# K^T V in column halves, states in quarters of the array, and weight rows loaded to match

## The chip, the cores and the metric

One core of one Trainium2 chip. The metric is the device time of one execution in microseconds (us), as the median of several runs.

## The reference

Eight batches of eight heads, 576 positions, head size 64: causal attention without softmax and with a decay per head, whose output, laid out as 4608 tokens of 512, goes through three up-projections with an elementwise maximum and one down-projection.

```python
scores = q @ k.T / sqrt(64)
ret = scores * where(i >= j, gamma[h] ** (i - j), 0)      # i, j positions
x = (ret @ v)                                            # heads side by side: 4608 x 512
h = maximum(maximum(x @ w1, x @ w2), x @ w3)             # 4608 x 768
out = h @ w_out                                          # 4608 x 512
```

The four weight matrices come as 64-bit floats; the kernel turns them into 32-bit ones itself.

## The kernel before

Tokens are cut into 36 chunks of 128 (`g`). For each chunk the kernel makes scores, multiplies them by the mask, multiplies with the decayed values `vd`, and adds the state of the earlier chunks times the queries. The state is a running sum of K^T V. Four chunks are a tile of 512 tokens for the projections (`up`, `downs`, in Strassen's form of seven products instead of eight). The attention of tile t+1 is spread over the projections of tile t.

```python
def state(g):                     # K^T V of a pair of heads as one 128x128 product
    ...
    kv = ps_r.tile([P, NP, P], FP32, tag="r", name="kv")
    for p in range(NP):           # NP = 4 pairs of heads
        nc.tensor.matmul(kv[:, p, :], lhsT=pair(kr, p)[r:], rhs=pair(vds[g], p)[r:], ...)     # L205
    ...                           # VectorE: + old state; GpSimd: * gs (which zeroes the off-diagonal blocks)

def values(*chunks):
    ...
    for p in range(NP):           # two heads beside each other in column halves
        for j in range(2):
            nc.tensor.matmul(o[g][D * j:D * (j + 1), p, :], lhsT=vr[:, 2 * p + j, :], rhs=st[:, j, p, :], ...)  # L226
    ...
            for p in range(NP):   # block-diagonal state of a pair, whole array
                nc.tensor.matmul(o[g][:, p, :old], lhsT=sd[:, p, :], rhs=qT[:, p, :old], ...)  # L234
    ...
def load_weights(n):
    ...
    nc.sync.dma_start(t[:].rearrange("p (dc f) -> p dc f", f=P),                               # one transfer a piece
                      WS[i][:, fb * P:(fb + 1) * P].rearrange("(dc p) f -> p dc f", p=P))
    ...
# in the steps of a tile, for each two chunks a, b:
at(m + 3, (state, a))
at(m + 4, (state, b))
at(m + 5, (values, a, b))
```

## Time and profile before

| | before |
|---|---|
| time | 820.41 us, median of 3 (819.88 to 820.86) |
| span in the profile | 818.6 us |
| stage 1, until the last weight is converted | 0 to 108.6 us |
| stage 2, to the end | 710.0 us |
| VectorE busy in 20.6 to 108.6 us | 86.7 of 88.0 us |
| granted clock | 1.00 throughout |

Two kinds of time are used. "Busy" is the time from an instruction's start to its end; for matmuls it contains latency and adds up to more than passes. "Start to start" is the time from a group's first start to the next group's first start; it is what the group costs in a full queue. A "record" is one matmul as the trace shows it; each product of 32-bit floats leaves two. The "mode" of the array is how it is divided: whole (128*128 in the lines), in column halves (128*64), row halves (64*128) or quarters (64*64). An "evacuation" is the operation that takes a result out of the bank of PSUM, the memory that matmuls write to, and so frees it. The prediction shows the lines of the profile on which both rest.

### The profile page before, as it was taken

How to read it: one execution, taken by the hardware profiler on the slowest of the kernel's cores; microseconds unless marked ns; L12 is line 12 of the kernel's file. 1: busy time of each engine (PE TensorE's matmuls, PEld its weight loads, DVE VectorE, ACT ScalarE, POOL GpSimd, SP SyncE). 2: the span in 40 equal slices, each digit the busy share in tenths (PEclk: the TensorE clock that was granted, in tenths of full speed). 3: DMA queues.
4: the chain of work that ended last, by engine and by line, in shares of the span. 5: the costliest groups of instructions: out<-in, count | busy, mean ns of one | idle time of the engine just before them, and what ended most of it. 6: DMA issues, size and time to landing. Idle time of an engine off the chain costs nothing.

```text
span 818.6 us, 12678 instructions
## 1 busy us (share of the span) xinstructions
PE 811.4 (99%) x4616; PEld 670.1 (82%) x4616; DVE 432.6 (53%) x805; ACT 173.7 (21%) x401; POOL 190.9 (23%) x182
## 2 busy tenths in 40 slices
PE   8999999999999999999999999999999999999998
PEld 7555457888888888888888888888888888888887
DVE  3999997454454535354445345553545344533341
ACT  2766521111111111110111111111111021111211
POOL 3645486112211130113021122102111302111000
PEclk9999999999999999999999999999999999999999
DMA  9966522333232323332224313333333232001001
GB/s 233 284 199 173 131 58 63 56 60 72 66 57 53 58 72 66 57 57 56 60 54 79 64 52 57 55 57 87 56 54 56 66 73 52 1 14 39 1 1 51
DMA packets 236094, 59.33 MB, mean 72 GB/s; under 512 B 217088, under 2 KB 234496, under 8 KB 236032
## 3 DMA queue, kind: packets, MB, share of 16 engines
q1 hardware_dynamic: 235888, 58.53, 32.0%
q8 instruction: 36, 0.59, 0.3%
q14 instruction: 26, 0.21, 0.1%
q10 hardware_dynamic: 144, 0.00, 0.0%
HBM read 49.03 MB, written 9.44 MB: 71 GB/s over the span
## 4 chain that ended last, share of the span: by engine, by line
PE 86%; DVE 6%; issue 2%; SPq 2%; DMA 2%; ACT 1%; POOL 0%; DVEq 0%; ACTq 0%
PE x L461 31%; PE z L461 15%; PE dx L334 10%; PE y L461 8%; PE dz L334 5%; PE o L226 3%; PE s L191 3%; PE o L234 3%; PE kv L205 3%; PE dy L334 3%; PE down L510 2%; DVE expo L413 2%; DVE frac L402 1%; SPq L160 1%; DVE mant L408 1%
## 5 line engine op out<-in xcount | busy, mean ns | idle before, releaser
L461 PE MATMUL x<-S,T 128*128 128x256 f32 x576 | 147.9, 379 | 0.0
L461 PEld LDWEIGHTS x<-S,T 128*128 128x128 f32 x576 | 109.1, 190 | 15.4 <-ACT u L466 0.3
L211 POOL TENSOR_TENSOR state<-state,gs 128x512 f32<-128x512 f32 x24 | 32.2, 1341 | 241.2 <-DVE state L210 237.3
L461 PE MATMUL x<-xT,w 128*128 128x256 f32 x288 | 75.6, 385 | 0.0
L491 DVE TENSOR_TENSOR tmp<-x,p 128x256 f32<-128x256 f32 x48 | 20.4, 424 | 102.8 <-PE x L461 102.8
L461 PE MATMUL x<-S,w 128*128 128x256 f32 x288 | 74.3, 380 | 0.0
L461 PE MATMUL y<-xT,w 128*128 128x256 f32 x288 | 73.9, 379 | 0.0
L461 PE MATMUL z<-S,w 128*128 128x256 f32 x288 | 73.9, 379 | 0.0
L461 PE MATMUL z<-xT,T 128*128 128x256 f32 x288 | 73.9, 379 | 0.0
L312 POOL TENSOR_TENSOR H<-h 128x256 f32<-128x256 f32 x24 | 20.5, 856 | 226.9 <-DVE h L504 226.9
L466 ACT COPY p<-x 128x256 f32<-128x256 f32 x72 | 26.8, 372 | 202.3 <-PE x L461 202.3
L519 PE MATMUL up<-xT,w 128*128 128x512 f32 x144 | 63.5, 595 | 0.2 <-POOL w L419 0.2
L238 DVE TENSOR_TENSOR xT<-o,gq 128x512 f32<-128x512 f32 x36 | 24.5, 689 | 69.9 <-PE o L234 63.9
L461 PEld LDWEIGHTS y<-xT,w 128*128 128x128 f32 x288 | 54.7, 190 | 7.4
L461 PEld LDWEIGHTS z<-S,w 128*128 128x128 f32 x288 | 54.7, 190 | 7.4
L461 PEld LDWEIGHTS z<-xT,T 128*128 128x128 f32 x288 | 54.5, 189 | 7.7
L461 PEld LDWEIGHTS x<-S,w 128*128 128x128 f32 x288 | 49.4, 189 | 13.2 <-issue 1.5
L461 PEld LDWEIGHTS x<-xT,w 128*128 128x128 f32 x288 | 52.1, 190 | 8.0 <-issue 0.5
L519 PEld LDWEIGHTS up<-xT,w 128*128 128x128 f32 x144 | 26.7, 190 | 31.4 <-issue 30.6
L194 DVE TENSOR_TENSOR st<-s,causal 128x512 f32<-128x512 f32 x72 | 44.9, 682 | 8.2 <-PE s L191 7.3
L466 ACT COPY u<-x 128x256 f32<-128x256 f32 x72 | 26.8, 372 | 100.2 <-PE x L461 95.7
L480 DVE TENSOR_TENSOR tmp<-y,p 128x256 f32<-128x256 f32 x48 | 20.4, 424 | 45.3 <-PE y L461 39.3
(92 smaller groups left out, 1218.9 us busy)
## 6 DMA issues: line engine op xcount, KB each, us to landing
bits<-in_moe_w_dram SPq DMA_DIRECT2D x18, 512.0 KB, 5.1
out_dram<-osb SPq DMA_DIRECT2D x35, 256.0 KB, 2.1
kraw<-in_k_dram SPq DMA_DIRECT2D x32, 256.0 KB, 3.0
vraw<-in_v_dram SPq DMA_DIRECT2D x32, 256.0 KB, 3.5
qraw<-in_q_dram SPq DMA_DIRECT2D x464, 16.0 KB, 1.8
kxraw<-in_k_dram SPq DMA_DIRECT2D x464, 16.0 KB, 1.8
bits<-in_moe_w_out_dram SPq DMA_DIRECT2D x6, 512.0 KB, 4.8
qraw<-in_q_dram SPq DMA_DIRECT2D x6, 256.0 KB, 5.6
```

Of the source, the lines that this page charges most:

```text
L191: nc.tensor.matmul(s[j][:, p, :], lhsT=kT[r, p, :], rhs=qT[r, p, :], start=True, stop=True)
L194: nc.vector.tensor_tensor(st[:, j], s[j][:], masks[start_of(g)][:].unsqueeze(1).to_broadcast([C, NP, C]), op=ALU.mult)
L205: nc.tensor.matmul(kv[:, p, :], lhsT=pair(kr, p)[r:], rhs=pair(vds[g], p)[r:], start=True, stop=True)
L211: nc.gpsimd.tensor_tensor(t[:], t[:], gs[:], op=ALU.mult)
L226: nc.tensor.matmul(o[g][D * j:D * (j + 1), p, :], lhsT=vr[:, 2 * p + j, :], rhs=st[:, j, p, :], start=(p == 0), stop=(before(g) == 0 and p ...
L234: nc.tensor.matmul(o[g][:, p, :old], lhsT=sd[:, p, :], rhs=qT[:, p, :old], start=False, stop=(p == NP - 1), skip_group_check=True)
L238: nc.vector.tensor_tensor(xT[t][:, :, i * C:(i + 1) * C], o[g][:], gq[:], op=ALU.mult)
L312: chores.append(lambda: (pool(s3, a11, a21, op=ALU.subtract), pool(s4, a12, s2, op=ALU.subtract)))
L334: nc.tensor.matmul(out[m], lhsT=hS[n](fp)[:, m * P:(m + 1) * P], rhs=late["T"][n][:, fp, :], start=first and fp == 0 and (m == 0 or last a ...
L461: nc.tensor.matmul(out[:], lhsT=w[:, d * P:(d + 1) * P], rhs=xS[t][n][:, d, :], start=first and d == 0, stop=d == 1, skip_group_check=True)
L466: nc.scalar.copy(c[:], src[:])
L519: nc.tensor.matmul(ps[:], lhsT=w_sb[i, fb][:, dc * P:(dc + 1) * P], rhs=xT[t][:, dc, :], start=(dc == 0), stop=(dc == NDC - 1))
```

## The change

Its intent: only the diagonal blocks of K^T V are wanted, and of the block-diagonal state half is zeros, so TensorE does twice the work needed. Per head, K^T V fits half of the array's columns, so two heads run side by side, and it is put directly behind the values, which use the same halves. The state times the queries is 64 by 64 per head, a quarter of the array, so four heads could run at once. For that, heads of both row halves must come to lie in each column half; the order of rows of x changes, and with it the rows of the three up weights and of the decay tables.

```diff
+    def state(g):
+            for h in range(H):
+                nc.tensor.matmul(kvs[g][half(h % 2), h // 2, :], lhsT=kr[r:, h, :], rhs=vds[g][r:, h, :], ...)
...
+    def head(c, n):
+        return NP * c + (n ^ c)
...
+        o = [pool.tile([P, len(chunks), NP // 2, C], FP32, tag=tag, name="o") for _ in range(2)]
+        (values: o[n % 2][half(c), m, n // 2, :] with h = head(c, n))
+        for g in new_states:
+            state(g)
-                    nc.tensor.matmul(o[g][:, p, :old], lhsT=sd[:, p, :], rhs=qT[:, p, :old], ...)
+                for n in range(NP):
+                    for c in range(2):
+                        h = head(c, n)
+                        r = half(h % 2)
+                        nc.tensor.matmul(o[n % 2][half(c), m, n // 2, :old], lhsT=states[g][r, h // 2, :],
+                                         rhs=qks[g]["q"][r, h // 2, :old], ...)
...
-                nc.sync.dma_start(t[:].rearrange("p (dc f) -> p dc f", f=P), ...)
+                for c, n in ((0, slice(0, NP)), (1, slice(0, NP, 2)), (1, slice(1, NP, 2))):
+                    h = slice(0, NP) if c == 0 else slice(head(c, n.start), H, 2)
+                    nc.sync.dma_start(blocks[half(c), n], heads[:, h])
...
+    def tables():                 # were two transfers, are six
+        for j in range(2):
+            yield gs[half(j)], state_decay[half(j), :, half(j)]
+        for c in range(2):
+            for b in range(2):
+                yield gq[half(c), b::2, :], out_decay[half(b ^ c), NP // 2 * c:NP // 2 * (c + 1), :]
...
-    state(0)                      # and so for chunks 1 to 3
-    values(0)
+    values([0], [0])
...
-            at(m + 3, (state, a))
-            at(m + 4, (state, b))
-            at(m + 5, (values, a, b))
+            at(m + 4, (decay_values, a + 2))
+            at(m + 5, (values, [a, b], [b, a + 2]))
```

(Cut: the smaller state and its evacuation `keep`, pool sizes, the passing of arguments.)

More of the change, by code (lines that the diff above doesn't have):

```diff
@@ L82 @@
     att = ctx.enter_context(tc.tile_pool(name="att", bufs=2))
-    stp = ctx.enter_context(tc.tile_pool(name="stp", bufs=3))
+    stp = ctx.enter_context(tc.tile_pool(name="stp", bufs=4))
     xpool = ctx.enter_context(tc.tile_pool(name="xpool", bufs=2))
@@ L98 @@
     gq = const.tile([P, NP, C], FP32, name="gq")
-    gs = const.tile([P, NP, P], FP32, name="gs")
+    gs = const.tile([P, NP, D], FP32, name="gs")
     nc.scalar.dma_start(gk[:], key_decay)
@@ L124 @@
         nc.gpsimd.memset(m[0:r, r:C], 0.0)
-    raws, vds, qks, sts, states = {}, {}, {}, {}, {}
+    raws, vds, qks, sts, states, kvs = {}, {}, {}, {}, {}, {}
     def spans(g):
@@ L156, in load @@
                 for t, what in between:
-                    nc.sync.dma_start(t[:], what)
+                    nc.sync.dma_start(t, what)
             t = raws[n, g] = raw.tile([C, H, D], FP32, tag=n, name=n + "raw", bufs=4 if n == "k" else 3)
@@ L195, in scores, with begins, half @@
                                     op=ALU.mult)
+    def begins(g):
+        return g + 1 < NG and start_of(g + 1) != 0
+    def half(j):
+        return slice(D * j, D * (j + 1))
     def state(g):
-        kr = raws.pop(("k", g))
-        if g + 1 == NG or start_of(g + 1) == 0:
-            return
-        r = start_of(g) or 0
-        kv = ps_r.tile([P, NP, P], FP32, tag="r", name="kv")
-        for p in range(NP):
-            nc.tensor.matmul(kv[:, p, :], lhsT=pair(kr, p)[r:], rhs=pair(vds[g], p)[r:], start=True, stop=True)
@@ L206, in state @@
-        t = states[g + 1] = stp.tile([P, NP, P], FP32, tag="state", name="state")
-        if start_of(g) is not None:
-            nc.vector.tensor_tensor(t[:], kv[:], gs[:], op=ALU.mult)
-        else:
-            nc.vector.tensor_tensor(t[:], kv[:], states[g][:], op=ALU.add)
-            nc.gpsimd.tensor_tensor(t[:], t[:], gs[:], op=ALU.mult)
+        kr = raws["k", g]
+        if begins(g):
+            r = start_of(g) or 0
+            pool, tag = (ps_r, "r") if g >= CPT else (ps_x, "x")
+            kvs[g] = pool.tile([P, NP, D], FP32, tag=tag, name="kv")
+            for h in range(H):
+                nc.tensor.matmul(kvs[g][half(h % 2), h // 2, :], lhsT=kr[r:, h, :], rhs=vds[g][r:, h, :],
+                                 start=True, stop=True)
@@ L213, with keep @@
+    def keep(g):
+        if begins(g):
+            kv = kvs.pop(g)
+            t = states[g + 1] = stp.tile([P, NP, D], FP32, tag="state", name="state")
+            if start_of(g) is not None:
+                nc.vector.tensor_tensor(t[:], kv[:], gs[:], op=ALU.mult)
+            else:
+                nc.vector.tensor_tensor(t[:], kv[:], states[g][:], op=ALU.add)
+                nc.gpsimd.tensor_tensor(t[:], t[:], gs[:], op=ALU.mult)
     xT, xS = {}, {}
-    def values(*chunks):
+    def head(c, n):
+        return NP * c + (n ^ c)
@@ L218, in before, with values @@
+    def values(chunks, new_states=()):
         def before(g):
             return C if start_of(g) is None else start_of(g)
-        o = {g: ps_r.tile([P, NP, C], FP32, tag="r", name="o") for g in chunks}
-        for g in chunks:
-            st, vr = sts.pop(g), vds.pop(g)
-            for p in range(NP):
-                for j in range(2):
-                    nc.tensor.matmul(o[g][D * j:D * (j + 1), p, :], lhsT=vr[:, 2 * p + j, :], rhs=st[:, j, p, :],
-                                     start=(p == 0), stop=(before(g) == 0 and p == NP - 1), skip_group_check=True)
@@ L228, in values @@
-        for g in chunks:
-            t, i = divmod(g, CPT)
-            qT, old = qks.pop(g)["q"], before(g)
-            if old > 0:
-                sd = states.pop(g)
-                for p in range(NP):
-                    nc.tensor.matmul(o[g][:, p, :old], lhsT=sd[:, p, :], rhs=qT[:, p, :old],
-                                     start=False, stop=(p == NP - 1), skip_group_check=True)
-            if i == 0:
-                xT[t] = xpool.tile([P, NDC, NT], FP32, tag="xT", name="xT")
-            nc.vector.tensor_tensor(xT[t][:, :, i * C:(i + 1) * C], o[g][:], gq[:], op=ALU.mult)
+        t, i = divmod(chunks[0], CPT)
@@ new lines, in values @@
+        pool, tag = (ps_r, "r") if t > 0 else (ps_y, "y")
+        o = [pool.tile([P, len(chunks), NP // 2, C], FP32, tag=tag, name="o") for _ in range(2)]
+        for m, g in enumerate(chunks):
+            for n in range(NP):
+                for c in range(2):
+                    h = head(c, n)
+                    nc.tensor.matmul(o[n % 2][half(c), m, n // 2, :], lhsT=vds[g][:, h, :],
+                                     rhs=sts[g][:, h % 2, h // 2, :], start=m == 0 and n < 2,
+                                     stop=before(g) == 0, skip_group_check=True)
@@ new lines, in values @@
+        for g in new_states:
+            state(g)
+        for m, g in enumerate(chunks):
+            old = before(g)
+            if old > 0:
+                for n in range(NP):
+                    for c in range(2):
+                        h = head(c, n)
+                        r = half(h % 2)
+                        nc.tensor.matmul(o[n % 2][half(c), m, n // 2, :old], lhsT=states[g][r, h // 2, :],
+                                         rhs=qks[g]["q"][r, h // 2, :old], start=False, stop=True,
+                                         skip_group_check=True)
@@ new lines, in values @@
+        if i == 0:
+            xT[t] = xpool.tile([P, NDC, NT], FP32, tag="xT", name="xT")
+        for b in range(2):
+            shape = [P, NP // 2, len(chunks), C]
+            nc.vector.tensor_tensor(
+                xT[t][:, b::2, i * C:(i + len(chunks)) * C].rearrange("p u (m c) -> p u m c", c=C),
+                o[b][:].rearrange("p m u c -> p u m c"), gq[:, b::2, :].unsqueeze(2).to_broadcast(shape), op=ALU.mult)
+        for g in new_states[:1]:
+            keep(g)
+        i += len(chunks) - 1
@@ L276, in load_weights @@
             else:
-                nc.sync.dma_start(t[:].rearrange("p (dc f) -> p dc f", f=P),
-                                  WS[i][:, fb * P:(fb + 1) * P].rearrange("(dc p) f -> p dc f", p=P))
+                heads = WS[i][:, fb * P:(fb + 1) * P].rearrange("(h p) f -> p h f", p=D)
+                blocks = t[:].rearrange("p (n f) -> p n f", f=P)
+                for c, n in ((0, slice(0, NP)), (1, slice(0, NP, 2)), (1, slice(1, NP, 2))):
+                    h = slice(0, NP) if c == 0 else slice(head(c, n.start), H, 2)
+                    nc.sync.dma_start(blocks[half(c), n], heads[:, h])
     late, chores = {}, deque()
@@ L557, in ffn @@
         yield
+    def tables():
+        for j in range(2):
+            yield gs[half(j)], state_decay[half(j), :, half(j)]
+        for c in range(2):
+            for b in range(2):
+                yield gq[half(c), b::2, :], out_decay[half(b ^ c), NP // 2 * c:NP // 2 * (c + 1), :]
     warm(6)
     load(0)
-    load(1, (gs, state_decay), (gq, out_decay))
+    load(1, *tables())
     load(2)
@@ L572 @@
     scores(0)
-    state(0)
     transposes(1)
-    values(0)
+    values([0], [0])
     decay_values(2)
     scores(1)
-    state(1)
     transposes(2)
-    values(1)
+    values([1], [1])
     decay_values(3)
     scores(2)
-    state(2)
     transposes(3)
     convert(2)
-    values(2)
+    values([2], [2])
     convert(2)
     scores(3)
-    state(3)
     decay_values(4)
     convert(2)
-    values(3)
+    values([3], [3])
     transposes(4)
@@ L601, in at @@
         def at(n, *what):
-            todo[n].extend(partial(step, *args) for step, *args in what if args[0] < NG)
+            for step, *args in what:
+                if step is values:
+                    if args[0][0] < NG:
+                        todo[n].append(partial(values, args[0], [g for g in args[1] if g < NG]))
+                elif args[0] < NG:
+                    todo[n].append(partial(step, *args))
         if t == 1:
@@ L606, in steps @@
             at(0, (load, b))
-            at(1, (scores, a), (state, a))
+            at(1, (scores, a), (state, a), (keep, a))
             at(2, (transposes, b), (decay_values, b), (load, c))
             at(3, (scores, b), (load_blocks, d, 0))
-            at(4, (state, b), (load_blocks, d, 1, 2))
-            at(5, (values, a, b), (load_blocks, d, 3), (load, d))
-            at(6, (transposes, c), (decay_values, c), (load_blocks, d + 1, 0))
+            at(4, (decay_values, c), (load_blocks, d, 1, 2))
+            at(5, (values, [a, b], [b, c]), (load_blocks, d, 3), (load, d))
+            at(6, (keep, c), (transposes, c), (load_blocks, d + 1, 0))
             at(7, (transposes, d), (decay_values, d), (load_blocks, d + 1, 1, 2))
             at(8, (scores, c), (scores, d), (load_blocks, d + 1, 3), (load, d + 1))
-            at(9, (state, c), (load_blocks, d + 2, 0, 1))
-            at(10, (state, d), (load_blocks, d + 2, 2))
-            at(11, (values, c, d), (load_blocks, d + 2, 3), (load, d + 2))
+            at(9, (load_blocks, d + 2, 0, 1))
+            at(10, (decay_values, d + 1), (load_blocks, d + 2, 2))
+            at(11, (values, [c, d], [d, d + 1]), (load_blocks, d + 2, 3), (load, d + 2))
             return todo
@@ L620, in steps @@
             a, b, m = CPT * t + n, CPT * t + n + 1, 6 * (n // 2)
-            at(m, (transposes, a), (decay_values, a), (load, a + 2))
+            at(m, (keep, a), (transposes, a), (load, a + 2))
             at(m + 1, (transposes, b), (decay_values, b))
             at(m + 2, (scores, a), (scores, b), (load, b + 2))
-            at(m + 3, (state, a))
-            at(m + 4, (state, b))
-            at(m + 5, (values, a, b))
+            at(m + 4, (decay_values, a + 2))
+            at(m + 5, (values, [a, b], [b, a + 2]))
         return todo
```

## The prediction

> **What bounds the kernel now.** I read the page first (busy shares, the 40 slices), then busy time by stage, the waits of TensorE, and last the matmul timeline at the places that the diff touches.
>
> ```profile
> PE 811.4 (99%) x4616; PEld 670.1 (82%) x4616; DVE 432.6 (53%) x805; ACT 173.7 (21%) x401; POOL 190.9 (23%) x182
> ...
> DVE  3999997454454535354445345553545344533341
> ```
>
> TensorE is busy for the whole span, but VectorE is full in the slices of roughly 20 to 130 us. The table by stage (stretch, its length, busy time of PE, PEld, DVE, ACT, POOL) makes it sharper:
>
> ```profile
> 20.00:108.00 88.00, 86.92 (x378) 46.34 (x374) 86.21 (x128) 55.72 (x85) 46.79 (x31) 1.00 0.69 187
> 108.00:130.00 22.00, 21.33 (x95) 11.79 (x96) 21.44 (x26) 1.76 (x3) 21.01 (x23) 1.00 0.29 74
> 130.00:818.60 688.60, 685.64 (x3977) 596.13 (x3975) 317.65 (x639) 110.76 (x305) 115.77 (x115) 1.00 0.26 53
> ```
>
> So there are two stages. Up to about 108 us, VectorE converts the 64-bit weights (86.2 of 88.0 us) and TensorE has to wait for what it makes; a faster TensorE gains nothing there. From 108 us on nothing holds TensorE back. The waits of the matmul row from 108 us to the end are one line:
>
> ```profile
> PE down L510 <- POOL w_out L419: 0.8, 1, 0.8
> ```
>
> The end is therefore set by how many array slots the second stage fills, about 706 us from 108.6 us on when I add up start-to-start times. I price everything by start-to-start, since a busy figure of a pipelined matmul (379 ns for one that starts every 216) is latency. In the timeline the next group's start closes a group; a matmul on 32-bit floats is two records, each with its own weight load:
>
> ```profile
> 156.27 1.05 PE L205 MATMUL kv<-vd,kraw 128*128 128x128 f32 x8
> 157.16 1.03 PE L461 MATMUL x<-xT,w 128*128 128x256 f32 x4
> ...
> 162.99 0.38 PE L461 MATMUL x<-S,w 128*128 128x256 f32 x1
> 163.30 1.97 PE L226 MATMUL o<-st,vd 128*64 128x128 f32 x32
> 165.20 1.16 PE L234 MATMUL o<-qT,state 128*128 128x128 f32 x8
> 166.19 0.38 PE L461 MATMUL x<-xT,w 128*128 128x256 f32 x1
> ```
>
> The reader is to see three prices. K^T V (L205): 8 records in 0.89 us, 111 ns each. Values in column halves (L226): 32 records in 1.90 us, 59 ns each; the single records show pairs 6 to 7 ns apart, one pair every 109 ns, so two halves really run at once. States with queries (L234) on the whole array: 8 in 0.99 us, and 16 in 1.89 us for two chunks. And a price for changing the array's shape: the full matmul before L226 takes 310 ns to the next start in place of 216 (+94), the first pair of L226 lasts 160 ns in place of 109 (+51), and L226 to L234 costs +93 and then +101.
>
> **What the Trainium skill says.** (1) "TensorEngine Tiling (Array Packing)", Tiling Modes, Key Properties: a change of tiling mode drains TensorE, while tiles of one mode load and multiply independently. The trace agrees: the 94 to 200 ns just named for a change, and pairs 7 ns apart within a mode. (2) "TensorE: Matmul & The Clock Gate", LDWEIGHTS: the load takes columns / 1.2 ns and does not depend on rows. In the load rows
>
> ```profile
> L226 PEld LDWEIGHTS o<-st,vd 128*64 128x64 f32 x576 | 31.2, 137 | 7.8 <-issue 6.5 <-DVE st L194 1.1 <-DVE state L210 0.2
> L234 PEld LDWEIGHTS o<-qT,state 128*128 128x128 f32 x256 | 30.0, 191 | 3.3 <-issue 3.3
> ```
>
> 128 columns cost 54 ns more than 64, as the page gives, and loads of 128 columns start every 111 to 112 ns. So L205 and L234 are paced by loads as much as by matmuls. (3) The same page, Back-to-back issue gap: columns / 2.4 + 2.5 ns, and a floor of about 25 ns per matmul. For these two-pass floats the trace has 216 ns at 256 columns and 109 at 128, which is the formula with two cycles a column; for 64 I take 56 to 57 ns. The floor has no witness in this trace: nothing here runs faster than 55 ns per record. (4) "TensorEngine Tiling", Gotcha 1: row tiles must not be in one PSUM bank at once. The diff obeys it: head(c, n) sends the two row halves that meet in one column half to two different banks.
>
> **The change part by part, in the second stage.**
>
> K^T V. Removed: 25 groups of 8 in the second stage (22.85 us by start-to-start: 22 at 0.891 and 3 half-chunk ones at 1.085). Of the full product only the two diagonal head blocks were ever used. Added: 16 records per chunk of 64 columns in and 64 out, two column halves side by side. A pair costs 57 ns by either load or matmul; 8 pairs are 0.456 us, and 25 chunks 11.4 us. They stand behind L226, in the same mode, so they add no change of shape. Gain **11.4 us**.
>
> States with queries. Removed: 15 groups in the second stage, 25.5 us (9 of 1.89, 3 of 1.835, 3 of 0.995). Added: twice the records, each in a quarter of the array. Four successive heads take four different quarters, so four records should share a 109 ns slot: 16 records a chunk are 4 slots, 0.437 us. 27 chunks give 11.8 us, less 3 x 0.21 for the chunks of which only 64 queries need a state, plus about 0.1 us at each of 15 entries: 12.7 us. Gain **12.8 us**.
>
> The price of quarters: the way out. L234 used to be in the same mode as the matmuls behind it; now there is one more change in each of 15 calls. Scores (L191), which also leave a tiled mode for the full array, show it:
>
> ```profile
> 142.09 2.06 PE L191 MATMUL s<-qT,kT 64*128 64x128 f32 x32
> 144.08 1.13 PE L461 MATMUL x<-xT,w 128*128 128x256 f32 x4
> ```
>
> The four L461 behind them take 0.967 us to the next start in place of 0.863, and the last score pair some 0.1 more: 0.2 us x 15 = **3.0 us lost**.
>
> Sum: 11.4 + 12.8 - 3.0 = 21.2 us.
>
> Other engines. The state's addition and scaling shrink from 512 to 256 columns (VectorE 687 ns towards the 424 that its 256-column additions take; GpSimd 1341 towards half). Neither is on the path after 108 us. Evacuations are again two of 512 columns per two chunks, but both now wait for the last of both chunks; that delays the sums for the next tile by 0.7 us or so. Those are wanted about 8 us later, so this is free. K^T V is taken a step earlier or later, with a whole up-projection unit (6 us) for its 1.07 us of decayed values.
>
> First stage. VectorE loses 0.26 us for each of some 7 states and pays 0.16 more for each of the first 4 evacuations (two of 256 columns for one of 512): about 1 us won, where it is full. Against it stands the transfer queue: 6 table transfers in place of 2, 3 for each of 18 weight pieces in place of 1, and an issue takes at least 0.43 us:
>
> ```profile
> 4.90 0.85 SPq L157 DMA_DIRECT2D gs<-in_state_decay_dram  x1
> 5.79 0.43 SPq L157 DMA_DIRECT2D gq<-in_out_decay_dram  x1
> ...
> 14.13 2.74 SPq L277 DMA_DIRECT2D bits<-in_moe_w_dram  x2
> ...
> 23.11 6.46 SPq L277 DMA_DIRECT2D bits<-in_moe_w_dram  x6
> ```
>
> Four more tables are +1.5 us of issue, but the queue stalls for 2.75 us right after them, with the transfer engines full, so most is absorbed, and 128 KB less is moved. A weight piece now costs 3 x 0.47 = 1.4 us to issue against the 1.1 to 1.4 us seen, so the first pieces come at most a microsecond later. Net of the stage: 0, give or take 1.5 us. 820.4 - 21.2 is 799.2; I state **800**, rounding towards a few unpriced fill slots.
>
> **The rivals.** (a) Quarters do not overlap fourfold. If loads or issue let only two records share a slot, L234 costs 8 slots a chunk, as before, and the extra change of mode makes that part a loss of 3 us: 820.4 - 11.4 + 3 = 812. For it: no four-way overlap and nothing under 55 ns per record is in this trace; a call now puts 96 matmuls and 96 loads in a row, where L226 had 32 and 32, so records may be issued too slowly (four loads and four matmuls per 109 ns are 14 ns each, where L226 needed 27). Against it: halves overlap perfectly by columns (L226) and by rows (L191), and starts 6 to 7 ns apart leave room for eight records in 109. (b) Only K^T V disappoints, since its matmuls are half as long: if a pair stays at 109 ns, its gain is 0 and the time 811. Against it: the second pair of loads of L226 starts 55 ns after the first. (c) The first stage grows: later weights delay VectorE, which is the bound there, and every lost microsecond stays. If all the added issue before the first weights were exposed, +2 to +4 us: 802 to 804. The 2.75 us stall speaks against it. (d) A new wait at the values call (K^T V before decayed values, or PSUM's four shared banks now holding two outputs and two states): 0.5 us in each of 15 calls would be +7, so 807. All their producers have most of a unit's 6 us, so I hold it unlikely.
>
> **Range and chances.** Faster by over 2% needs less than 804.0. The main path (both overlaps work) has 0.65 to 0.7 and ends at 797 to 803; (a) or (b) has about 0.2 and ends at 808 to 812; (c) and (d) push a little more over 804. Slower than 836 would need a failure of a kind I see no sign of. Range 796 to 811; faster 0.66, same 0.31, slower 0.03.
>
> **What would show it.** K^T V at about 28 ns per record start-to-start, 0.46 us per chunk; L234's successor at about 27 ns per record, 1.0 us per two chunks; each call still followed by a slow first full matmul (0.1 us more); TensorE's waits after 108 us still near 0; the first `down` still at about 103 us and the rest of the program 21 us shorter. Wrong if the records of quarters sit at 55 ns, if K^T V pairs stay near 109, if waits for a state, for decayed values or for a PSUM buffer appear on TensorE, or if the conversion of weights ends later than before.

## The result, and the profile after

The changed kernel takes 806.97 us (median of 4, 804.83 to 808.08) against 820.23 us (median of 4, 819.88 to 820.86). The ratio is 0.9834, 95% interval 0.9811 to 0.9858: better by 1.7%, short of 2%. Ratios here are the mean time of one kernel's runs over the mean of the other's of the same rounds, so they are not quite the ratio of the quoted medians.

The array did what was hoped. One values call for two chunks, in the matmul timeline of the kernel before (columns: start, duration to the last end, engine, line, operation, tile, count):

```profile
204.79 1.97 PE L226 MATMUL o<-st,vd 128*64 128x128 f32 x32
206.69 2.05 PE L234 MATMUL o<-qT,state 128*128 128x128 f32 x16
208.58 0.38 PE L334 MATMUL dx<-To,H 128*128 128x256 f32 x1
```

and the same call after:

```profile
207.48 1.97 PE L244 MATMUL o<-st,vd 128*64 128x128 f32 x32
209.28 1.10 PE L211 MATMUL kv<-vd,kraw 128*64 128x64 f32 x32
210.31 1.10 PE L256 MATMUL o<-qT,state 64*64 64x128 f32 x32
211.35 0.48 PE L367 MATMUL dx<-To,H 128*128 128x256 f32 x1
```

Read starts against starts. K^T V of two chunks takes 1.03 us (209.28 to 210.31), where it took 2 x 0.89. States take 1.04 us (210.31 to 211.35) against 1.89. In the single records, K^T V goes in pairs 6 to 7 ns apart every 58 ns, and the states go four at a time, 6 to 7 ns apart, every 109 ns.

The stages of the kernel after (stretch, length, busy time of PE, PEld, DVE, ACT, POOL with counts, granted clock, DMA share, GB/s) show where the rest went:

```profile
23.00:113.00 90.00, 84.04 (x430) 43.41 (x422) 85.26 (x132) 55.41 (x84) 48.48 (x32) 0.98 0.74 182
113.00:134.60 21.60, 21.58 (x118) 11.03 (x119) 19.82 (x25) 1.76 (x3) 19.92 (x22) 0.93 0.34 82
134.60:803.10 668.50, 665.40 (x4369) 575.57 (x4367) 305.96 (x639) 110.76 (x305) 105.00 (x114) 1.00 0.27 55
```

| us, profiled runs | before | after | difference |
|---|---|---|---|
| VectorE starts converting weights | 20.63 | 22.91 | +2.3 |
| last weight converted (end of stage 1) | 108.62 | 112.96 | +4.3 |
| first matmul of the Strassen products | 129.86 | 134.60 | +4.7 |
| from the first Strassen product to the end | 688.7 | 668.5 | -20.2 |
| span | 818.6 | 803.1 | -15.5 |

So the array gained 20.2 us from the first Strassen product on, and the start gave 4.7 back. Three things are new in the start. The first is the transfer queue, in the timeline of its issues:

```profile
5.28 1.52 SPq L157 DMA_DIRECT2D gs<-in_state_decay_dram  x2
6.84 2.56 SPq L157 DMA_DIRECT2D gq<-in_out_decay_dram  x4
...
17.26 4.12 SPq L311 DMA_DIRECT2D bits<-in_moe_w_dram  x6
...
26.88 11.83 SPq L311 DMA_DIRECT2D bits<-in_moe_w_dram  x18
```

The two tables took 1.33 us to issue and now take 4.1; the first weights are issued at 17.26 us, not 14.13; the next six pieces take 11.8 us, not 6.5. The second is a wait of VectorE inside the conversion, in its timeline (in brackets the idle time before it and its cause):

```profile
31.33 0.76 DVE L263 TENSOR_TENSOR xT<-o,gq 128x256 f32<-128x256 f32 x2 [2.96 <-PE o L256]
```

The third is the clock. The kernel before was granted 1.00 all along. This one has two stretches of 3.4 us at half of it, called slow stretches below:

```profile
27.50:30.90 3.40, 3.30 (x41) 3.13 (x44) 0.87 (x3) 1.44 (x2) 1.03 (x2) 0.50 0.80 202
112.80:116.20 3.40, 3.18 (x4) 1.50 (x5) 3.13 (x5) 0.58 (x1) 2.86 (x5) 0.50 0.21 32
```

The second of these lies in stage 2, where TensorE sets the end: 3.4 us at half speed costs an estimated 1.7. The experiments bear this out: from the conversion's end to the first Strassen product, the profiled runs without a slow stretch there (e1, e6, e8, e12) take 20.06 to 20.12 us, those with one (the change, e2, e3, e5) 21.44 to 21.76. The first lies on the work that VectorE waits for at 28 to 31 us. The Trainium skill ("TensorE: Matmul & The Clock Gate", Part 1: The HAM clock gate) says that the clock halves after an idle window of about 3.4 us and that windows run freely; the length of 3.4 us and the share of 0.50 agree. I had read it and saw no reason to use it, since nothing in the trace before was throttled.

### The profile page after: what moved, and what is told of

Same layout as the page of the kernel before. It is cut to its first block, busy times and chain, and to the rows that moved or that the text cites. A ratio compares the mean times of both kernels' runs of the same rounds, so it can differ in the third digit from the quotient of the medians.

```text
span 803.1 us, 13762 instructions
## 1 busy us (share of the span) xinstructions
PE 789.4 (98%) x5128; PEld 646.0 (80%) x5128; DVE 417.4 (52%) x809; ACT 173.8 (22%) x401; POOL 179.9 (22%) x182
## 5 line engine op out<-in xcount | busy, mean ns | idle before, releaser
L263 DVE TENSOR_TENSOR xT<-o,gq 128x512 f32<-128x512 f32 (+1 forms) x40 | 23.7, 632 | 85.2 <-PE o L256 83.8
L222 POOL TENSOR_TENSOR state<-state,gs 128x256 f32<-128x256 f32 x24 | 20.7, 862 | 166.7 <-DVE state L221 166.7
```

The lines of the kernel that those rows point to most:

```text
L222: nc.gpsimd.tensor_tensor(t[:], t[:], gs[:], op=ALU.mult)
L263: nc.vector.tensor_tensor(xT[t][:, b::2, i * C:(i + len(chunks)) * C].rearrange("p u (m c) -> p u m c", c=C), o[b][:].rearrange("p m u c - ...
```

## The experiments

Theories. **Transfers**: more and smaller transfers delay the first weights and what VectorE does from there. **Order**: K^T V behind the values lengthens the path from masked scores to the evacuation in the first chunks, and VectorE stands behind it. **Clock**: TensorE's new idle time lowers its clock, where that costs time. For the array: whether the gain hangs on the place of K^T V, and on the order of the quarters. The profiled positions (conversion end and so on) are quoted from one profiled run each. Medians of different submissions were taken on different chips.

| run | correct | median us (runs) | ratio [95%] | conversion start / end | conversion end to end of program |
|---|---|---|---|---|---|
| the change | yes | 806.97 (4) | 0.9834 [0.9811, 0.9858] | 22.91 / 112.96 | 690.1 |
| e1_tables_whole | yes | 803.16 (4) | 0.9797 [0.9784, 0.9809] | 20.46 / 111.36 | 689.8 |
| e2_weights_whole | no | 804.10 (4) | 0.9800 [0.9788, 0.9813] | 21.33 / 112.10 | 690.3 |
| e3_both_whole | no | 802.59 (5) | 0.9782 [0.9769, 0.9795] | 20.14 / 109.75 | 690.9 |
| e4_before_split | yes | 823.25 (6) | 1.0039 [1.0026, 1.0051] | 22.75 / 111.97 | 710.0 |
| e5_two_transfers | yes | 801.11 (5) | 0.9762 [0.9737, 0.9787] | 20.50 / 110.06 | 690.5 |
| e6_early_states | yes | 800.96 (5) | 0.9759 [0.9740, 0.9779] | 21.25 / 109.91 | 689.3 |
| e7_states_apart | yes | 809.73 (4) | 0.9872 [0.9853, 0.9892] | 22.20 / 110.86 | 696.8 |
| e8_same_quarter | yes | 803.62 (4) | 0.9807 [0.9783, 0.9831] | 22.02 / 112.93 | 689.7 |
| e9_late_fill | yes | 805.04 (4) | 0.9812 [0.9793, 0.9832] | 21.64 / 112.34 | 693.2 |
| e10_both_fill | yes | 803.93 (4) | 0.9798 [0.9785, 0.9812] | 19.85 / 108.10 | 692.7 |
| e11_early_states_fill | yes | 803.75 (5) | 0.9800 [0.9787, 0.9814] | 20.90 / 109.70 | 693.0 |
| e12_fill_other_bank | yes | 799.38 (5) | 0.9748 [0.9735, 0.9761] | 20.04 / 108.85 | 688.3 |

### Whole transfers again: tables, weights, both

```diff
 # e1_tables_whole: constants laid out beforehand in the new order
-        for j in range(2): yield gs[half(j)], ...      # and four pieces of gq
+        yield gs[:], state_decay
+        yield gq[:], out_decay
 # e2_weights_whole: one transfer a piece, old row order (wrong result on purpose)
+                nc.sync.dma_start(t[:].rearrange("p (dc f) -> p dc f", f=P), ...)
 # e3_both_whole: both
```

> The changed kernel with the two decay tables laid out beforehand in the new order, so that each is one transfer again (256 KB and 128 KB) in place of four and two pieces of 64 KB. Transfer theory (the 4.3 us by which the weight conversion ends late come from more and smaller transfers at the start): the two table issues take about 1.3 us in place of 4.1, the first weights are issued near 14.2 us in place of 17.3, the conversion ends near 110 us, time 803 to 804. Order theory (the late end comes from K^T V standing behind the values in the first chunks, so that TensorE waits for decayed values): no change, 807.

> The changed kernel with each weight piece loaded in one transfer and in the old row order (a wrong result on purpose; all work is the same). Transfer theory: the first two pieces are issued in 2.7 us in place of 4.1 and the next six in about 6.5 in place of 11.8, the conversion ends 1 to 2 us earlier, time 805 to 806. Order theory: no change, 807.

> Both at once (again a wrong result on purpose). Transfer theory: the gains add; conversion ends near 108.5 us, time 799 to 802, the 800 of the prediction. Order theory: 807, with the matmul waits of several microseconds before 28 us still there.

Measured: 803.2, 804.1 and 802.6 us. The conversion ends 1.6, 0.9 and 3.2 us earlier than in the changed kernel. In the issue timeline with both whole, the tables and the first weights are back where they were:

```profile
5.07 1.02 SPq L157 DMA_DIRECT2D gs<-in_state_decay_dram  x1
6.14 0.43 SPq L157 DMA_DIRECT2D gq<-in_out_decay_dram  x1
...
14.78 1.35 SPq L307 DMA_DIRECT2D bits<-in_moe_w_dram  x2
```

The rival that expected no change falls. The positions are the cleaner evidence here, since the medians also hold the clock (0.995 to 0.998 in these runs, 0.992 to 0.995 in the changed kernel's). But the times were somewhat above what the transfer theory expected of the third run (799 to 802), and the conversion end of the first was 111.4 us, not 110: in all three VectorE still waits about 3 us near 26 us (2.95 in the third), and slow stretches of the clock remain: two in the second and third, one of 6.8 us from 23.7 us in the first.

### The kernel before, with nothing but the split transfers

```diff
-    load(1, (gs, state_decay), (gq, out_decay))
+    load(1, *tables())            # gs in 2 pieces, gq in 4, same bytes and places
-                nc.sync.dma_start(t[:]..., ...)
+                for c, n in ((0, slice(0, NDC)), (1, slice(0, NDC, 2)), (1, slice(1, NDC, 2))):
+                    nc.sync.dma_start(blocks[D * c:D * (c + 1), n], rows[D * c:D * (c + 1), n])
```

> The kernel before with nothing changed but the transfers: the tables in 2 and 4 pieces, each weight piece in 3, same bytes and same places. Result correct. Transfer theory: conversion ends 4 us later, time 824 to 825. Order theory: 820 to 821.

Measured: 823.25 us, ratio 1.0039 (interval above 1). The conversion ends at 111.97 us, 3.35 later, and the span is 3.36 longer: all of it stays. Its queue shows the same issues as the changed kernel:

```profile
5.43 1.51 SPq L157 DMA_DIRECT2D gs<-in_state_decay_dram  x2
6.99 2.53 SPq L157 DMA_DIRECT2D gq<-in_out_decay_dram  x4
...
16.12 4.81 SPq L280 DMA_DIRECT2D bits<-in_moe_w_dram  x6
```

With the attention untouched, the splitting alone costs some 3.2 us. This is the strongest evidence for the transfer theory, and it agrees with the 3.2 us by which whole transfers end the conversion earlier in the changed kernel. But the profiled run also has a slow stretch, near 16 us:

```profile
14.60:17.90 3.30, 3.30 (x20) 2.97 (x20) 0.69 (x1) 1.00 (x2) 2.19 (x2) 0.50 1.11 252
```

Three of the six runs had its clock of 0.998 (mean 824.3 us), the other three one of 1.0 (mean 822.3). So the splitting costs about 2.2 us where the clock does not fall, and the 3.2 us hold a share of the clock's. It also shows that late data alone can bring a slow stretch, with the array work of the kernel before. The Trainium skill points the same way: "DMA: Bandwidth & Descriptors", Rules for kernel authors, advises one transfer over 128 partitions and not two over disjoint halves, since both spread over the same engines. I had not consulted it for the prediction.

### A correct version with fewer transfers

```diff
-        return NP * c + (n ^ c)
+        return NP * c + n
-            for n in range(NP):
+            for s in range(NP):
                 for c in range(2):
+                    n = s ^ c
-                for c, n in (... three ...):
+                for c in range(2):
+                    nc.sync.dma_start(blocks[half(c)], heads[:, NP * c:NP * (c + 1)])
 # and the tables whole, as in e1
```

The exchange of neighbours is moved from the layout to the order of the matmuls. The queue of the array is the same, but the weights' rows come in two plain runs.

> A correct version with fewer transfers: heads in column half c are 4c+n without the exchange of neighbours, so a weight piece is two transfers, tables are one each, and the matmuls walk n = s xor c so that the quarters follow each other exactly as in the changed kernel (same row half now always writes the same bank). Transfer theory: conversion ends between 109.8 us (whole pieces, wrong result) and 111.4 us (tables whole only), time 801 to 803.5. If the order of quarters or the bank choice of the change mattered: states with queries slower than 27 ns per record, time 805 or more.

Measured: 801.11 us (796.61 to 802.61), as the transfer theory expected, conversion end 110.06. One run had a granted clock of 1.0 and took 796.61; the others had 0.994 to 0.998. A slow stretch of 3.4 us is worth an estimated 1.7 us where it costs fully; the two runs at 0.998 were 4.0 and 4.5 us longer than the one at 1.0, so one slow stretch does not explain it. What else differed is not on record, since only one run was profiled.

### K^T V of the first chunks put back

```diff
     scores(0)
+    state(0)
+    keep(0)
     transposes(1)
-    values([0], [0])
+    values([0])                   # and so for chunks 1 to 3
```

> The same version, with K^T V of the first four chunks put back before the transposes of the next chunk, as in the kernel before (only there; later calls keep it beside the values). Order theory for the about 1.1 us that whole transfers left unexplained (109.75 against 108.62 us): conversion ends about 1 us earlier than in the version with two transfers. Rival (the rest is the throttled clock or the pieces of the weights): conversion ends within 0.3 us of it.

Measured: 800.96 us against 801.11, no difference. VectorE's wait fell from 2.92 to 1.58 us and the conversion became 0.9 us shorter (88.66 us against 89.56), but in the profiled run it also began 0.75 us later, so its end did not move (109.91). Order is visible in the wait, but this run does not show that it is worth anything in time. Inconclusive.

### K^T V in steps of its own

```diff
-            at(m, (keep, a), (transposes, a), (load, a + 2))
-            at(m + 5, (values, [a, b], [b, a + 2]))
+            at(m + 3, (state, a), (keep, a))
+            at(m + 4, (state, b), (keep, b), (decay_values, a + 2))
+            at(m + 5, (values, [a, b], []))
```

> The changed kernel with K^T V still per head in column halves, but in steps of its own between whole-array matmuls, as the kernel before had it. If the gain of K^T V depends on standing beside the values: each group then pays an entry and an exit of the tiled mode, about 0.38 us more for each of 25 groups, time 815 to 818, a group near 0.84 us with its changes of mode against 0.89 before. If shorter records alone made the gain: 806 to 808.

Measured: 809.73 us, less loss than I expected. One group alone:

```profile
156.81 1.03 PE L494 MATMUL x<-S,w 128*128 128x256 f32 x4
157.76 0.69 PE L211 MATMUL kv<-vd,kraw 128*64 128x64 f32 x16
158.38 1.13 PE L494 MATMUL x<-xT,w 128*128 128x256 f32 x4
```

It takes 0.62 us from start to start, the four full matmuls before it 0.96 and those behind it 0.97 in place of 0.86: 0.81 us in all, against 0.89 before the change. From the first Strassen product to the end this kernel takes 676.4 us, 7.9 more than the changed one, 0.33 us for each of 24 groups. So the place beside the values makes most of K^T V's gain; the shorter records alone gain next to nothing. My total was wrong because stage 1 went the other way: the conversion ended 2.1 us earlier than in the changed kernel and no slow stretch of the clock fell into stage 2. I did not settle why the conversion ended earlier.

### Two heads in a row in one quarter

```diff
-                for n in range(NP):
-                    for c in range(2):
+                for c in range(2):
+                    for n in (0, 2, 1, 3):
```

> The changed kernel with the heads of the state products in another order: each quarter gets two heads in a row before the next quarter starts (same records, same result). If records start in program order (one that finds its quarter busy holds back those behind it): about 1.3 us per chunk in place of 0.45, 20 us or more lost, time 825 to 832. If a record may pass one that waits for its quarter: no change, 805 to 808.

Measured: 803.62 us. The states of two chunks take 1.10 us (208.78 to 209.88) against 1.04:

```profile
208.78 1.17 PE L256 MATMUL o<-qT,state 64*64 64x128 f32 x32
209.88 0.91 PE L367 MATMUL dx<-To,H 128*128 128x256 f32 x3
```

In the single records four still share each slot of 109 ns, now 13 to 14 ns apart. So the theory of strict order falls: a record does get past one that waits for its quarter, and the careful order of the quarters is worth 0.06 us a call. The same is seen in the changed kernel near 29 us, where K^T V records start before the last record of the values that precede them in the program:

```profile
29.00 0.42 PE L211 MATMUL kv<-vd,kraw 128*64 128x64 f32 x2
29.20 0.42 PE L244 MATMUL o<-st,vd 128*64 128x128 f32 x1
```

This run also warns of something. Its transfers are those of the changed kernel and its array work is slightly longer, yet its median is 3.3 us lower. Its clock was 0.998 in three of four runs, where the changed kernel's was 0.992 to 0.995. And its one slow stretch lay at 16.0 to 19.4 us, so VectorE waited only 0.67 us for the values of chunk 3:

```profile
30.70 0.76 DVE L263 TENSOR_TENSOR xT<-o,gq 128x256 f32<-128x256 f32 x2 [0.67 <-PE o L256]
```

Yet its conversion ended at 112.93 us, as in the changed kernel (112.96), where this wait was 2.96 us. VectorE's own busy time in the conversion was 87.4 us here and 85.3 there, for a reason that I did not find. So a shorter wait at this place need not end the conversion earlier. Differences of 1 to 3 us are therefore read from positions in the profile, not from medians.

### Filling the idle time: into a bank that was held

```diff
 # e9_late_fill (on e5): in the first down product
+            if t == 0 and m == 0 and fb >= NF - 2:
+                warm(8 if fb == NF - 2 else 4)      # throw-away matmuls on the identity, bank of ps_y
 # e10_both_fill: also, before the values of chunk 3
+    warm(12, ps_x, "x")
 # e11_early_states_fill: both (8 in the second place) on e6
```

> The version with two transfers, plus 12 throw-away matmuls on the identity (0.22 us each) before the last two blocks of the first down product, where TensorE sits idle for some 2.5 us waiting for the last converted weights. Clock theory (the low clock of 3.4 us that begins near 110 us follows from this idle time and falls on work that sets the end): that slow window is gone, conversion end to end of program 1.5 us shorter (near 689 in place of 690.5), median 799 to 800 against 801. Rival (the slow window comes from elsewhere): window still there, 801 to 803.

> As the one before, plus 12 throw-away matmuls before the values of chunk 3, where TensorE waits 3.5 us for the masked scores. Clock theory: the slow window near 25 us goes too, the values, K^T V and states of chunk 3 take half the time, VectorE's wait of 2.9 us for them near 26 us shrinks to about 1, conversion ends 1.5 to 2 us earlier (near 108.3), granted clock 1.0, time 796.5 to 798.5, like the one run of 796.61 that had clock 1.0. Rival (that wait is set by transfers): conversion end near 110, time 799 to 801.

> The same filling on the version that has K^T V of the first four chunks before the next transposes. If order and clock add up: VectorE's wait near 27 us under 1 us, conversion end 107.5 to 108.5, time 795.5 to 797.5. If the order matters only through the clock: the same as the one before, within 0.5 us.

Measured: 805.0, 803.9 and 803.8 us, all worse than the unfilled 801.1 and 801.0 (e10_both_fill by little: its interval touches that of e5_two_transfers). The late filling was built badly. In the timeline of e10_both_fill it waits for an evacuation by VectorE (L558, a maximum) to free its bank, and comes after the idle time that it was to fill:

```profile
107.40 3.66 PE L113 MATMUL warm<-ident 128*128 128x128 f32 x16 [2.07 <-DVE h L558]
110.90 1.02 PE L546 MATMUL down<-w_out,h 128*128 128x512 f32 x2
```

From the conversion's end on, the three need 692.7 to 693.2 us in place of 690.5. The early filling did work: with it (e10_both_fill) VectorE's wait near 26 us is 0.65 us in place of 2.92, no slow stretch lies there, and the conversion ends at 108.10 us, the earliest of all runs (it also began earliest, at 19.85).

```profile
26.82 0.75 DVE L265 TENSOR_TENSOR xT<-o,gq 128x256 f32<-128x256 f32 x2 [0.65 <-PE o L258]
```

On top of it, early states (e11_early_states_fill) bring nothing in time: 803.75 against 803.93. In its profile this wait fell further, to 0.27 us, but VectorE waited 1.86 us for weights, which it did not in e10_both_fill. So the run is no clean test of the order.

### The same filling into a free bank

```diff
-                warm(8 if fb == NF - 2 else 4)
+                warm(7 if fb == NF - 2 else 3, ps_r, "r")
```

> The version with two transfers, the 12 throw-away matmuls before the values of chunk 3, and 7 and 3 (in place of 8 and 4) before the last two blocks of the first down product, now into a PSUM bank that nobody holds: in the two fillings before, these had to wait for a maximum of VectorE that frees their bank, so they came after the idle time and cost 2.5 us. Clock theory: conversion ends near 108.1 us as in the run with both fillings, no slow window near 110 us, from there to the end 688.5 to 689.5, time 798 to 799.5. If the late slow window is not from idle time: it stays, and the time is 800 to 801.5. If the filling itself delays: from the conversion's end to the program's end more than 690.5.

Measured: 799.38 us (798.34 to 800.95), ratio 0.9748 [0.9735, 0.9761], correct: the lowest median, and faster than both kernels. Its interval overlaps that of e5_two_transfers, so the two are not told apart by their times alone. Its two stages and the wait that was 2.96 us:

```profile
20.00:108.90 88.90, 88.41 (x498) 48.23 (x493) 85.67 (x132) 55.46 (x84) 47.40 (x32) 1.00 0.76 185
108.90:797.20 688.30, 685.13 (x4486) 585.89 (x4486) 326.45 (x663) 112.73 (x308) 124.92 (x135) 1.00 0.27 56
```

```profile
27.66 0.76 DVE L265 TENSOR_TENSOR xT<-o,gq 128x256 f32<-128x256 f32 x2 [0.66 <-PE o L258]
```

The granted clock is 0.999 to 1.0 in all five runs, no slow stretch is left in the profile, and stage 2 takes 688.3 us, 2.2 less than in e5_two_transfers (which lost 1.7 to its slow stretch at 110 us). Both slow stretches went when the idle time before them was filled, as the clock theory says. Slow stretches come and go between runs even unfilled (the profiled runs of e1, e6, e8 have none after the conversion), so the five runs weigh more here than the one profile: all five are at 0.999 or above, against one of five in e5_two_transfers. The useless work pays by avoiding slow stretches; that it is free is not shown, since the one run of e5_two_transfers at a clock of 1.0 took 796.61 us, less than any of these five.

## Why the prediction was right or wrong

The time, 807.0 us, lies within 796 to 811, but in the part to which I gave less weight: I put 0.66 on faster by over 2%, and the ratio is 0.9834. That it lies in the range is in part luck: the upper part was held open above all for rivals (a), (b) and (d), and none of them happened.

- **K^T V, 11.4 us gained: right in mechanism, close in size.** From the first Strassen product on, its groups fell from 21.96 to 12.83 us by start to start. A pair takes 58 ns (I took 57). The groups now also carry the way out of their mode, which the values carried before (26.57 to 25.46 us).
- **States in quarters, 12.8 us gained: right.** In the same stretch 23.65 to 12.57 us. Four records share 109 ns. Rival (a), no fourfold overlap, is out.
- **One more change of mode, 3.0 us lost: right in kind.** The full matmuls behind the calls are 1.07 us longer in this stretch (14 calls), and the last group of four takes about 0.1 us more each time. The balance of all these terms, 9.13 + 11.08 + 1.11 - 1.07, is 20.25 us, and the stretch did shorten by 20.2. In the same 24 groups K^T V should have gained 11.0 us, so it and the values together (10.24) came 0.8 us short.
- **21.2 us in stage 2: right.** From the conversion's end to the program's end it went from 710.0 to 690.1 us, 19.9. With the 1.7 us of the slow stretch added back it is 21.6. The profiled runs with this array work and no slow stretch there show 689.8 (e1), 689.7 (e8, its other order included), 689.3 (e6) and 688.3 (e12): gains of 20.2 to 21.7.
- **"Net of the stage: 0, give or take 1.5 us": wrong; this is the step that failed.** Stage 1 became 4.3 us longer, so one of the prediction's own signs of being wrong, a later end of the conversion, appeared. I priced an issue at "at least 0.43 us", the lowest I saw, and let a stall of 2.75 us absorb the extra issues. In fact the six table pieces of 64 KB took 0.60 to 0.88 us each to issue, 4.1 us in all; the first two weight pieces, six transfers, took 4.12 us, 2.1 a piece in place of the 1.4 that I had priced; the weights came 3.1 us later, and little was absorbed. e4_before_split puts the splitting at 3.2 to 3.4 us on its own, 2.2 in its runs at full clock. Rival (c) named this and gave it +2 to +4, but as the case where all were exposed; it was the ordinary case.
- **The clock: missing from the prediction.** No rival named it. TensorE now has idle time in the start, and it is then granted half its clock for 3.4 us at a time. Part of this idle time comes from the later data, since e4_before_split has a slow stretch too; how much comes from the smaller array work is argued, not shown. In the profiled run the clock cost about 1.7 us in stage 2 and a share of VectorE's 2.96 us wait in stage 1. Whether that share ended stage 1 later is open: e10_both_fill says yes, e8_same_quarter no. The other three runs of the changed kernel, at clocks of 0.992 and 0.993, were 1.3 to 3.3 us longer than the profiled one at 0.995; where their slow stretches lay was not recorded.
- **Rival (d), new waits in the values calls: did not happen.** After the conversion TensorE has no wait of note; its waits from 100 us on are one line:

```profile
PE down L543 <- POOL w_out L452: 2.1, 2, 1.3
```

- **Reading (4), "The diff obeys it": too generous.** Heads 0 and 5 of a chunk, which run at once, lie in different row halves and both write `o[0]`, which is one bank; heads 1 and 4 both write `o[1]`. The page as cited there makes no exception for different column halves. The result was correct, and the states took 12.57 us, as in e5_two_transfers (12.58), where each row half has a bank of its own. So nothing was lost by it here.

What stays open: how the remaining microsecond of stage 1 (109.75 us with whole transfers against 108.62 before) divides between order and clock. e6_early_states did not separate them; e10_both_fill and e12_fill_other_bank, which keep the new order and end at 108.10 and 108.85 once TensorE's idle time is filled, suggest the clock, but do not prove it: each is one profiled run, and VectorE's own busy time in the conversion varies by more than that microsecond between profiled runs in which that work is the same (84.7 us in e5_two_transfers, 85.9 in e10_both_fill, 87.4 in e8_same_quarter).

## What to carry to other kernels

Packing small products into parts of the array works nearly to the full factor, if products of one shape of tiling stand together; alone between whole-array work, two changes of mode eat the gain. A change that is priced in the stage where the engine is the bound also has to be priced in the other stage: here a layout that helped the array cost three times as many transfers where transfers set the start. When a part of the work of the bounding engine goes away, look at where it will now be idle, since its clock may fall there and be low in the work that follows.

## What the Trainium skill lacked or had wrong

- "TensorE: Matmul & The Clock Gate", Part 3, says that matmuls are in program order in start and end. Here records of another part of the array got past waiting ones: two K^T V records start at 29.00 us, before a values record at 29.20 that precedes them in the program; and two heads in a row per quarter cost 1.10 us in place of 1.04, not three times as much.
- "TensorEngine Tiling (Array Packing)", Key Properties, says that a change of mode drains TensorE but gives no price. Here: +94 ns before it and a first pair of 160 ns in place of 109, or 0.81 us for a group of K^T V alone that costs 0.46 us (8 pairs of 58 ns) in a stream.
- No page gives the rates of two-pass 32-bit floats in tiles. ("Two-pass" because each product leaves two records.) Here: a pair of column halves of 64 columns every 58 ns, four quarters of 128 columns every 109 ns.
- "DMA: Bandwidth & Descriptors", Rules for kernel authors, is right that halves of the partitions in two transfers don't pay; the price is not there. Here: pieces of 64 KB took 0.60 to 0.88 us each to issue, against 0.85 and 0.43 for the two whole tables of 256 KB, and splitting cost 3.2 us of 820 (2.2 at full clock).
- "TensorE: Matmul & The Clock Gate", Why this matters for your kernels, advises against idle gaps of over about 3 us between bursts. That is not enough here: the half clock from 112.8 us came after waits of 2.1 us in two pieces, the longest 1.3 us.
